# Loading the first batch in order of use, and keeping six partial sums of the first weight open while the values slip in between

## The chip, the cores and the metric

The kernel runs on one core of one Trainium2 chip; the other cores are idle. The metric is the device time of the whole kernel in microseconds (us). The time of one run lies about 1.8 us above the span of the profile, which goes from the first to the last instruction. Time before: 408.8 us, the median of three runs (408.26 to 409.0).

The change touches only the first 45 us.

## The reference, cut to what matters

Linformer attention, then a feed-forward layer with the maximum over three products:

```python
k_proj = einsum('ks,bhsd->bhkd', E, k)        # E, F: 64 x 1024
v_proj = einsum('ks,bhsd->bhkd', F, v)        # q, k, v: 8 x 8 x 1024 x 64
attn   = softmax(q @ k_proj.T / sqrt(64))
x      = (attn @ v_proj), heads side by side  # 8192 x 512
h      = max(x @ w1, x @ w2, x @ w3)          # 512 x 768 each
out    = h @ w_out                            # 768 x 512
```

All inputs and outputs are float32.

## The kernel before

The operands of every matmul are held in bf16; sums and maxima stay in float32. Each load of q, k, v and of the weights changes float32 to bf16 on the way. The Trainium skill ("DMA: Bandwidth & Descriptors", section "SWDGE vs HWDGE vs iDMA") says that a cast during a DMA is to be had from GpSimd only. The kernel keeps to this: all such loads are issued by GpSimd and stand in one queue, q0, with 28.31 MB written. In the trace of the kernel before, the loads of the first batch land in the order in which they are issued (the first at 6.2 us, k of the next batch at 43.4 us). That order is a matter of choice.

The work goes batch by batch (8), each in two chunks of 512 rows. In the first chunk of the first batch TensorE waits for loads; later everything is there in time. w1, w2, w3 are the three weights; each comes in two halves of its rows, that is of the contraction (`ct` 0, 1 and `ct` 2, 3). A column tile `jt` (6 of them) needs 4 matmuls per weight, one for each `ct`. Before, the loads were issued like this (the calls are shortened):

```python
    load_q(LO, first half)      # q, heads 0-3
    load_kv(1, LO)              # k, heads 0-3
    load_kv(2, 0:2); load_kv(2, 2:4)          # v, first two pairs of heads
    make_identity(nc, ident)
    load_w(0, 0)                # first half of w1
    load_q(HI, first half); load_kv(1, HI)    # q and k, heads 4-7
    load_w(1, 0)                # first half of w2
    load_kv(2, V2); load_kv(2, V3)            # v, last two pairs
    load_w(1, 1); load_w(0, 1)  # second halves of w2, of w1
    load_w(2, 0); load_w(2, 1)  # w3
    load_q(ALL, rest)           # q for the second chunk
    # ... w_out, then k of batch 1
```

The first chunk follows that order. TensorE attends to heads 0 to 3 and does `ct` 0 and 1 of w1. It copies these half sums out of PSUM, attends to heads 4 to 7, and does most of w2. Then it returns to w1, and the half sums are added on VectorE, or copied by ScalarE and added by GpSimd:

```python
        for ct in range(2):
            for jt in jts:
                up_mm(h[jt][0], 0, 0, 0, jt, (ct,), last=1)
                if ct == 1:
                    copy("sv"[jt % 2], s1[:, jt], *h[jt])
        then(0)                 # attention of heads 4-7
        # ... w2, ct 0 to 2, into six banks
        for jt in jts:
            t, ns = bank()
            up_mm(t, 0, 0, 0, jt, (2, 3), first=2)
            # ... add to s1; w2, ct 3; maximum
        for jt in jts:
            t, ns = bank()
            up_mm(t, 2, 0, 0, jt, range(NCT))       # w3
            most(hTs[0, 0][:, jt, :], t, ns, s1[:, jt])
            then(5 + jt)        # 5, 6: transposes of the rest of q
```

`idle(n)` issues n warm-up matmuls on zeroes. PSUM is the memory into which TensorE writes its sums; its 8 banks are dealt one at a time (`bank`) or as an aligned pair (`two`). The other names in the code: `q_duo` and `qp` transpose q, `k_pair` and `v_pair` project k and v, `scores` and `exps` are the product of q and k and its exponential, `z` makes the inverse of the softmax sums, `x` multiplies with v and scales. The number in brackets is a pair of heads (for `q_duo` two pairs). `then(key)` does the work that is listed under that key.

The softmax here doesn't subtract the row's maximum and nothing guards it: scores larger than these inputs give would overflow.

## Time and profile before

| | before |
|---|---|
| time, median of 3 runs | 408.8 us |
| span of the profiled run | 407.8 us |
| TensorE busy | 393.8 us (97%) |
| TensorE idle in 0 to 35 us | 6.2 us |
| casting queue | about 206 GB/s written, unbroken from 9 us to beyond 43 us |

Of the page of the kernel before: the span, the busy time of the engines, and the clock that was granted to TensorE in 40 slices, in tenths.

```profile
span 407.8 us, 6116 instructions
...
PE 393.8 (97%) x2452; PEld 180.4 (44%) x2497; DVE 202.3 (50%) x311; ACT 192.9 (47%) x281; POOL 34.9 (9%) x46
...
PEclk9899999999999999999999999999999999999999
```

TensorE (PE) is what is full.

Stretches of 5 us of the kernel before: the stretch, its length, then busy time and number of instructions of PE, weight loads, VectorE, ScalarE, GpSimd, then the granted clock, the DMA share and GB/s written.

```profile
25.00:30.00 5.00, 3.93 (x38) 1.83 (x38) 1.97 (x4) 0.01 (x1) 0.00 (x0) 1.00 1.19 206
30.00:35.00 5.00, 5.00 (x26) 2.13 (x27) 4.10 (x7) 1.77 (x3) 2.97 (x3) 1.00 1.33 204
35.00:40.00 5.00, 4.95 (x54) 2.29 (x54) 5.00 (x9) 1.09 (x2) 2.63 (x3) 1.00 1.24 207
```

From 30 us on TensorE has hardly a gap. So only the time at which it gets there can change.

The timeline of PE of the kernel before (start, duration, line, operation, shapes, count; in brackets the idle time before it and what ended that). L406 projects k, L460 is the up product, L288 projects v, L299 transposes q:

```profile
10.51 0.69 PE L406 MATMUL banks<-efT,k_t 128*64 128x64 bf16 x32 [1.61 <-DMA k_t<-in_k_dram]
...
16.45 2.76 PE L460 MATMUL banks<-xT,w_sb 128*128 128x512 bf16 x11
...
27.46 0.64 PE L288 MATMUL banks<-v_t,efT 128*64 128x128 bf16 x16 [0.80 <-DVE xT L257]
...
29.02 5.92 PE L460 MATMUL banks<-xT,w_sb 128*128 128x512 bf16 x25
34.88 0.64 PE L299 MATMUL banks<-ident,q_t 128*64 128x128 bf16 x16
```

Three things are to be seen. TensorE waits 1.61 us for the first half of k. At 27.46 us it waits 0.80 us for VectorE, because six banks are taken and the remaining pair is still being read. And the first transposes of the rest of q, which stand behind the first column tile of w3, begin when that tile is done, at 34.9 us.

The granted clock comes in stretches of 3.41 us. The two around 12.5 us, of the kernel before (the clock is the column after GpSimd):

```profile
9.08:12.49 3.41, 1.47 (x44) 1.12 (x45) 0.45 (x2) 0.86 (x2) 1.19 (x2) 1.00 1.23 208
12.49:15.91 3.42, 3.33 (x45) 2.02 (x41) 1.03 (x3) 2.59 (x5) 1.67 (x3) 0.50 1.29 201
```

A stretch in which TensorE worked for 1.47 us is followed by one at half clock.

The chain of waits of the same run (start, duration, what):

```profile
18.38 1.89 DVE s L99 x3
20.27 0.39 DVE qT L99
...
20.79 0.23 DVE kpT L99
21.01 0.04 issue
21.05 0.43 PE banks L207 x8
```

Three of the six copies of half sums are done by VectorE, ahead of what the attention of heads 4 to 7 needs from it. In the timeline TensorE waits 0.46 us for VectorE at 21.05 us.

### The profile page before, as it was taken

Reading aid. Unit: us, or ns where it says so; the run is one execution under the profiler, and the core shown is the slowest. Engines: PE = TensorE matmul, PEld = TensorE weight load, DVE = VectorE, ACT = ScalarE, POOL = GpSimd, SP = SyncE. Lnnn points to the kernel's source line nnn. Section 1 sums busy time; section 2 is a strip of 40 time slices with the busy share of each in tenths; the row PEclk is TensorE's granted clock in tenths of the full one; section 3 lists DMA queues with packets and bytes.
Section 4 is the critical chain, followed back from the end, with each engine's and each line's share of the span. In section 5 each row is a group of like instructions: output and inputs, shape, how many; then the busy total and the mean of one; then the engine's idle time right before and its main releaser. Section 6 shows DMA issues by size and latency. Waiting matters only on the chain.

```text
span 407.8 us, 6116 instructions
## 1 busy us (share of the span) xinstructions
PE 393.8 (97%) x2452; PEld 180.4 (44%) x2497; DVE 202.3 (50%) x311; ACT 192.9 (47%) x281; POOL 34.9 (9%) x46
## 2 busy tenths in 40 slices
PE   7879999999999999999999999999999999999995
PEld 2534454344444544444544445444544444444443
DVE  1429665473465527636453565525464363525251
ACT  2432537623764266547445555537535555432322
POOL 7325002002000200200010002000000000000000
PEclk9899999999999999999999999999999999999999
DMA  9999939959926994893799109960520202020202
GB/s 152 206 207 206 220 98 145 251 122 127 244 42 161 191 247 123 121 242 54 182 184 204 52 13 243 203 161 0 123 87 0 104 2 103 2 103 0 104 0 104
DMA packets 58492, 52.30 MB, mean 128 GB/s; under 512 B 25952, under 2 KB 54112, under 8 KB 58464
## 3 DMA queue, kind: packets, MB, share of 16 engines
q0 software_dynamic: 28496, 28.31, 43.8%
q1 hardware_dynamic: 29824, 23.46, 17.9%
q8 instruction: 19, 0.31, 0.3%
q10 hardware_dynamic: 144, 0.13, 0.1%
q14 instruction: 9, 0.07, 0.1%
HBM read 57.15 MB, written 16.78 MB: 181 GB/s over the span
## 4 chain that ended last, share of the span: by engine, by line
PE 91%; DMA 3%; ACT 2%; DVE 2%; issue 1%; POOL 0%; ACTq 0%; DVEq 0%; POOLq 0%
PE banks L460 60%; PE banks L586 19%; PE banks L227 4%; PE banks L288 4%; DMA k_t<-in_k_dram 2%; PE banks L207 2%; PE banks L299 1%; ACT zl L240 1%; DVE xT L257 1%; ACT pT L218 1%; DMA out_dram<-o_sb 0%; DVE s L99 0%; ACT zi L246 0%; DVE m L551 0%; ACT o_sb L99 0%
## 5 line engine op out<-in xcount | busy, mean ns | idle before, releaser
L460 PE MATMUL banks<-xT,w_sb 128*128 128x512 bf16 x1118 | 255.1, 379 | 2.1 <-issue 0.5
L460 PEld LDWEIGHTS <-w_sb 128*128 128x128 bf16 x1152 | 109.4, 98 | 137.0 <-issue 10.7
L551 DVE TENSOR_TENSOR m<-banks,h1s 128x512 f32<-128x512 f32 x90 | 62.0, 689 | 86.1 <-ACT h1s L547 54.7
L547 ACT COPY h1s<-banks 128x512 f32<-128x512 f32 x90 | 52.5, 583 | 92.5 <-PE banks L460 89.2
L586 PE MATMUL banks<-wout_sb,hT 128*128 128x512 bf16 x369 | 84.8, 379 | 0.7 <-DVE hT L470 0.2
L257 DVE TENSOR_TENSOR xT<-banks,zi 128x1024 bf16<-128x1024 f32 (+1 forms) x36 | 39.8, 1106 | 78.4 <-ACT zi L246 53.7
L470 DVE TENSOR_TENSOR hT<-banks,m 128x512 bf16<-128x512 f32 x90 | 62.3, 692 | 10.1 <-PE banks L227 0.5
L99 ACT COPY o_sb<-banks 128x512 f32<-128x512 f32 (+1 forms) x60 | 34.9, 581 | 53.0 <-PE banks L586 53.0
L586 PEld LDWEIGHTS <-hT 128*128 128x128 bf16 x378 | 36.0, 98 | 45.5 <-issue 3.1
L240 ACT ACTIVATE zl<-banks 128x1024 f32<-128x1024 f32 (+1 forms) x36 | 33.5, 931 | 30.8 <-PE banks L227 30.6
L218 ACT ACTIVATE pT<-banks 128x1024 bf16<-128x1024 f32 (+1 forms) x36 | 33.2, 931 | 9.7 <-PE banks L207 9.7
L246 ACT ACTIVATE zi<-zl 128x1024 f32<-128x1024 f32 (+1 forms) x36 | 34.6, 962 | 1.1
L196 POOL DMA_DIRECT2D q_t<-in_q_dram x7 | 6.2, 883 | 194.1 <-DMA qT<-q_p 72.1
L288 PEld LDWEIGHTS <-efT 128*64 128x64 bf16 x288 | 14.5, 116 | 4.5 <-issue 4.1
L227 PE MATMUL banks<-pT,ones 64*64 64x512 bf16 (+1 forms) x144 | 14.0, 379 | 1.5 <-ACT pT L218 0.9
L207 PE MATMUL banks<-qT,kpT 64*64 64x512 bf16 (+1 forms) x144 | 13.1, 360 | 0.9 <-DVE kpT L99 0.5
L227 PE MATMUL banks<-pT,vp 64*64 64x512 bf16 (+1 forms) x144 | 13.4, 359 | 0.4 <-DVE vp L99 0.4
L99 DVE CAST vp<-banks 64x256 bf16<-64x256 f32 (+1 forms) x18 | 7.1, 397 | 10.7 <-PE banks L288 7.1
L288 PE MATMUL banks<-v_t,efT 128*64 128x256 bf16 (+1 forms) x176 | 10.7, 271 | 0.9 <-DVE xT L257 0.8
L227 PEld LDWEIGHTS <-ones 64*64 64x64 bf16 x144 | 4.5, 103 | 15.4 <-issue 15.3
L99 ACT CAST vp<-banks 64x256 bf16<-64x256 f32 x14 | 5.1, 365 | 7.3 <-PE banks L288 7.1
L99 DVE COPY q_p<-q_t 128x1024 bf16<-128x1024 bf16 x24 | 8.5, 419 | 0.0
(47 smaller groups left out, 106.7 us busy)
## 6 DMA issues: line engine op xcount, KB each, us to landing
out_dram<-o_sb SPq DMA_DIRECT2D x30, 512.0 KB, 3.1
k_t<-in_k_dram POOLq DMA_DIRECT2D x7, 1024.0 KB, 14.0
q_t<-in_q_dram POOLq DMA_DIRECT2D x7, 1024.0 KB, 9.6
v_t<-in_v_dram POOLq DMA_DIRECT2D x7, 1024.0 KB, 18.5
w_sb<-in_moe_w_dram POOLq DMA_DIRECT2D x6, 384.0 KB, 14.8
k_t<-in_k_dram POOLq DMA_DIRECT2D x2, 512.0 KB, 11.0
v_t<-in_v_dram POOLq DMA_DIRECT2D x4, 256.0 KB, 11.5
wout_sb<-in_moe_w_out_dram POOLq DMA_DIRECT2D x1, 768.0 KB, 16.3
```

Source lines behind the costliest of these rows:

```text
L99: done = {"v": nc.vector.tensor_copy, "s": nc.scalar.copy, "g": nc.gpsimd.tensor_copy}[eng](out=o, in_=i)
L218: nc.scalar.activation(out=pTs[b, g, lo], in_=t, func=AF.Exp, scale=scale)
L227: nc.tensor.matmul(out=t[hp * HALF:(hp + 1) * HALF, c, 0:nsi * HALF], lhsT=w(rows, hp), rhs=p[rows, hp, :], start=True, stop=True,)
L240: nc.scalar.activation(out=zl, in_=t, func=AF.Ln)
L246: nc.scalar.activation(out=zi, in_=zl, func=AF.Exp, scale=-1.0)
L257: nc.vector.tensor_tensor(out=xTs[b][:, g, lo:lo + nsi, :].rearrange("a (c s) p -> a c (s p)", c=2), in0=t, in1=zi, op=ALU.mult,)
L288: nc.tensor.matmul(out=t[hh * HALF:(hh + 1) * HALF, 0:width], lhsT=efT[:, si, kv - 1, :], rhs=qkv[b][kv][:, heads[hh], si, :], start=(si = ...
L460: nc.tensor.matmul(out=h, lhsT=w_sb[i][:, ct, jt * P:(jt + 1) * P], rhs=xTs[b][:, ct, ch * SPC:(ch + 1) * SPC, :], start=(ct == first), st ...
L470: nc.vector.tensor_tensor(out=o, in0=h, in1=other, op=ALU.max)
L547: nc.scalar.copy(out=h1s, in_=h[0][0])
L551: nc.vector.tensor_tensor(out=m12, in0=h[1][0], in1=h1s, op=ALU.max)
L586: nc.tensor.matmul(out=o_ps, lhsT=hTs[b, ch][:, jt, tt * P:(tt + 1) * P], rhs=wout_sb[:, jt, :], start=(jt == 0), stop=(jt == NJT - 1),)
```

## The change

The intent: let all attention inputs come first, so that the attention of all eight heads is done before the up product starts. Then w1 can run through in one go, with its six banks open over all four `ct`, without copies of half sums, additions or a second visit; the six copies are made of the full sums of w1 at its end instead. The last two pairs of v, and what of the softmax depends on them, slip in between its `ct` steps while the second half of w1 is on its way. The diff, cut to its core:

```diff
     load_q(LO, slice(0, SPC))
     load_kv(1, LO)
+    load_q(HI, slice(0, SPC))
+    load_kv(1, HI)
     load_kv(2, slice(0, 2))
     load_kv(2, slice(2, 4))
 # ... cut
     load_w(0, 0)
-    load_q(HI, slice(0, SPC))
-    load_kv(1, HI)
-    load_w(1, 0)
     load_kv(2, V2)
     load_kv(2, V3)
+    load_w(0, 1)
+    load_w(1, 0)
     load_w(1, 1)
-    load_w(0, 1)
     load_w(2, 0)
+    load_q(ALL, slice(SPC, SI))
     load_w(2, 1)
-    load_q(ALL, slice(SPC, SI))
 # ... cut: k of batch 1 is issued with the rest of its loads, but first
-    for g in range(2):
+    for g in (0, 1):
         exps(0, g, *C0, scores(0, g, *C0))
+    idle(2)
+    z(0)
+    q_duo(1)
+    z(1)
+    idle(2)
+    k_pair(2)
+    k_pair(3)
+    for g in (2, 3):
+        exps(0, g, *C0, scores(0, g, *C0))
     idle(1)
-    z(0)
     v_pair(0)
-    z(1)
-    idle(1)
+    z(2)
     x(0)
     v_pair(1)
+    z(3)
     x(1)
 # ... cut: the old up_first
+        for ct in range(NCT):
             for jt in jts:
-                up_mm(h[jt][0], 1, 0, 0, jt, (ct,))
+                up_mm(h[jt][0], 0, 0, 0, jt, (ct,))
+                if ct == NCT - 1:
+                    copy("sv"[jt % 2], hs[:, jt], *h[jt])
+                if jt == 2 or jt == NJT - 1:
+                    then((0, ct, jt))
+        for i in (1, 2):
+            for jt in jts:
+                t, ns = bank()
+                up_mm(t, i, 0, 0, jt, range(NCT))
+                most(hs[:, jt] if i == 1 else hTs[0, 0][:, jt, :], t, ns, hs[:, jt])
+                then((i, jt))
 # ... cut
-                    1: [lambda: v_pair(2)],
-                    2: [lambda: x(2), lambda: v_pair(3)],
-                    3: [lambda: x(3)],
-                    5: [qp(0, (0, 1), *c1)],
-                    6: [qp(0, (2, 3), *c1)],
+                    (0, 1, 2): [lambda: v_pair(2)],
+                    (0, 1, 5): [lambda: x(2), lambda: v_pair(3)],
+                    (0, 2, 2): [lambda: x(3)],
+                    (2, 0): [qp(0, (0, 1), *c1)],
+                    (2, 1): [qp(0, (2, 3), *c1)],
```

Before, the rest of q came behind all of w3; after, it comes ahead of w3's second half.

More of the change, by code (lines that the diff above doesn't have):

```diff
@@ L169 @@
     load_w(0, 0)
-    load_q(HI, slice(0, SPC))
-    load_kv(1, HI)
-    load_w(1, 0)
     load_kv(2, V2)
     load_kv(2, V3)
+    load_w(0, 1)
+    load_w(1, 0)
     load_w(1, 1)
-    load_w(0, 1)
     load_w(2, 0)
+    load_q(ALL, slice(SPC, SI))
     load_w(2, 1)
-    load_q(ALL, slice(SPC, SI))
     nc.gpsimd.dma_start(out=wout_sb, in_=moe_w_out.rearrange("(jt p) m -> p jt m", p=P))
-    def load_k1():
-        nonlocal k_t1
-        k_t1 = loads.tile([P, H, SI, D], BF16, name="k_t")
-        nc.gpsimd.dma_start(out=k_t1, in_=view(k, 1))
-    k_t1 = None
     def load(b):
         tiles = tuple(
-            loads.tile([P, H, SI, D], BF16, name=nm) if b > 1 or i != 1 else k_t1
-            for i, nm in enumerate(("q_t", "k_t", "v_t"))
+            loads.tile([P, H, SI, D], BF16, name=nm) for nm in ("q_t", "k_t", "v_t")
         )
         qkv[b] = tiles
-        for i in ((0, 2) if b == 1 else (0, 1, 2)):
+        for i in ((1, 0, 2) if b == 1 else (0, 1, 2)):
             dma = nc.gpsimd.dma_start(out=tiles[i], in_=view((q, k, v)[i], b))
@@ L431, with z, x @@
     C0 = (0, SPC)
+    def z(g):
+        invert(0, g, *C0, sums(0, g, *C0))
+    def x(g):
+        scale_x(0, g, *C0, values(0, g, *C0))
     idle(11)
@@ L437 @@
     k_pair(1)
-    for g in range(2):
+    for g in (0, 1):
         exps(0, g, *C0, scores(0, g, *C0))
-    def z(g):
-        invert(0, g, *C0, sums(0, g, *C0))
-    def x(g):
-        scale_x(0, g, *C0, values(0, g, *C0))
+    idle(2)
[7 more added lines that the diff above has]
+        exps(0, g, *C0, scores(0, g, *C0))
     idle(1)
-    z(0)
     v_pair(0)
-    z(1)
-    idle(1)
+    z(2)
     x(0)
     v_pair(1)
+    z(3)
     x(1)
@@ L479, in then @@
                 f()
-        s1 = ffn_sb.tile([P, NJT, CHUNK], FP32, name="s1", bufs=1)
-        s2 = ffn_sb.tile([P, NJT, CHUNK], FP32, name="s2", bufs=1)
+        hs = ffn_sb.tile([P, NJT, CHUNK], FP32, name="hs", bufs=1)
         hTs[0, 0] = ffn_sb.tile([P, NJT, CHUNK], BF16, name="hT")
         jts = range(NJT)
-        def six():
-            return [(t[:, n], ns[n:n + 1]) for t, ns in (two(), two(), two()) for n in (0, 1)]
-        h = six()
-        for ct in range(2):
+        h = [(t[:, n], ns[n:n + 1]) for t, ns in (two(), two(), two()) for n in (0, 1)]
@@ L491, in up_first @@
+        for ct in range(NCT):
             for jt in jts:
-                up_mm(h[jt][0], 0, 0, 0, jt, (ct,), last=1)
-                if ct == 1:
-                    copy("sv"[jt % 2], s1[:, jt], *h[jt])
-        then(0)
-        load_k1()
-        h = six()
-        for ct in range(2):
-            for jt in jts:
-                up_mm(h[jt][0], 1, 0, 0, jt, (ct,))
-            then(1 + ct)
-        for jt in jts:
-            up_mm(h[jt][0], 1, 0, 0, jt, (2,))
-            if jt == 2:
-                then(3)
@@ L506, in up_first @@
-        for jt in jts:
-            t, ns = bank()
-            up_mm(t, 0, 0, 0, jt, (2, 3), first=2)
-            if jt % 2:
-                copy("s", s2[:, jt], t, ns)
-                nc.gpsimd.tensor_tensor(
-                    out=s1[:, jt], in0=s1[:, jt], in1=s2[:, jt], op=ALU.add
-                )
-                added = clock["s"] + 1.3
-            else:
-                nc.vector.tensor_tensor(out=s1[:, jt], in0=t, in1=s1[:, jt], op=ALU.add)
-                added = runs("v", clock["pe"], 0.69, ns)
-            up_mm(h[jt][0], 1, 0, 0, jt, (3,))
-            if jt % 2 == 0:
-                most(s1[:, jt], *h[jt], s1[:, jt], added)
-            elif jt > 2:
-                most(s1[:, jt - 2], *h[jt - 2], s1[:, jt - 2], last)
-            if jt % 2:
-                last = added
@@ L525, in up_first @@
-        most(s1[:, 5], *h[5], s1[:, 5], last)
-        then(4)
-        for jt in jts:
-            t, ns = bank()
-            up_mm(t, 2, 0, 0, jt, range(NCT))
-            most(hTs[0, 0][:, jt, :], t, ns, s1[:, jt])
-            then(5 + jt)
+                up_mm(h[jt][0], 0, 0, 0, jt, (ct,))
[4 more added lines that the diff above has]
+        for i in (1, 2):
+            for jt in jts:
+                t, ns = bank()
+                up_mm(t, i, 0, 0, jt, range(NCT))
+                most(hs[:, jt] if i == 1 else hTs[0, 0][:, jt, :], t, ns, hs[:, jt])
+                then((i, jt))
@@ L673 @@
                 c1 = (SPC, SPC)
-                def attend():
-                    q_duo(1)
-                    k_pair(2)
-                    k_pair(3)
-                    for g in (2, 3):
-                        exps(0, g, *C0, scores(0, g, *C0))
-                    idle(2)
-                    for g in (2, 3):
-                        z(g)
-                up_first({
-                    0: [attend],
-                    1: [lambda: v_pair(2)],
-                    2: [lambda: x(2), lambda: v_pair(3)],
-                    3: [lambda: x(3)],
-                    5: [qp(0, (0, 1), *c1)],
-                    6: [qp(0, (2, 3), *c1)],
-                    7: [sc(0, 0, *c1)],
-                    8: [sc(0, 1, *c1)],
-                    10: [za(0, 0, *c1), sc(0, 2, *c1)],
+                up_first({
+                    (0, 1, 2): [lambda: v_pair(2)],
[3 more added lines that the diff above has]
+                    (2, 1): [qp(0, (2, 3), *c1)],
+                    (2, 2): [sc(0, 0, *c1)],
+                    (2, 3): [sc(0, 1, *c1)],
+                    (2, 5): [za(0, 0, *c1), sc(0, 2, *c1)],
                 })
```

## The prediction

> **What bounds the kernel now.** From about 29 to 402 us TensorE is dense: the page has PE busy 393.8 of 407.8 us, and the table of stretches shows 4.85 to 5.0 us of each 5 us from 30 us to 65 us. Behind the first stage nothing is changed but bank numbers. So only the moment when TensorE can run without gaps can move.
>
> Before that the casting queue binds: the DMA view shows about 206 GB/s (written bytes) unbroken from 9 to beyond 43 us. Landings (issue plus time to landing): q low 6.2, k low 10.5, v0 11.7, v1 13.0, first half of w1 14.9, q high 16.4, k high 19.9, first of w2 21.7, v2 23.1, v3 24.3, second of w2 26.2, second of w1 28.1, w3 30.0 and 31.9, rest of q 34.5, w_out 38.3, next k 43.4. TensorE idles 6.2 us in 0 to 35 us (stretches), 1.6 of it before the first k projection. In the timeline the first column tile of w3 ends at 34.95 us.
>
> **What changes.** No byte and no up matmul goes (72 before and after); warm-up matmuls 21, then 22 (+0.2 us). Removed: three VectorE adds (0.69 us each), three ScalarE copies (0.59) and three GpSimd adds (3.9 in all), off the chain. k, q and v come before the weights: w1's first half moves from 14.9 to about 19 us (2.49 MB instead of 1.70 MB, at 206 GB/s).
>
> **New order, estimated from these durations.** k high lands at 14.3 to 15.3; softmax of groups 2 and 3 (ScalarE 0.6 us a step) ends by about 18; v0, v1 at 16 to 17; w1's first steps start at 19 to 19.5. v2 (20.3), v3 (21.6) and w1's second half (23.5) are slipped in; only one bank pair is left, so v_pair(3) waits 0.8 us for VectorE, as now. w1 ends near 27.3. w2's second half lands at 28.1, so TensorE waits 0.5 us; w2 ends near 32.9. w3's second half, now behind the rest of q, lands where the rest of q does now, 34.5 us: the bytes in front are the same. w3's first tile ends at 34.5 + 2 x 0.216 + 0.05 = 35.0 us, against 34.95. The remaining work is the same.
>
> So the early gain is given back to one weight half: about 0, perhaps 0.3 us from a less loaded VectorE (5.0 of 5.0 us busy in 35 to 40 us now).
>
> **The clock.** The Trainium skill ("TensorE: Matmul & The Clock Gate", Part 1) says activity in a free-running window of about 3.4 us sets full or half clock. The trace agrees: 9.1 to 12.5 us has 1.53 us of PE work, and 12.5 to 15.9 us ran at 0.5. I expect one or two such windows after; 1.6 us of slack before w3's second half absorbs a second.
>
> **Prediction: 408.6 us, 407.3 to 410.3. Faster by over 2%: 0.01; within 2%: 0.98; slower by over 2%: 0.01.**
>
> **What would show it.** First up matmul near 19 us (16.45 now); w1 done near 27; PE waits of 0.5 us at 28 and of 1 to 1.5 us for w_sb ending near 34.5; w3's first tile ending at 34.5 to 35.3; next k at 43.4; PE busy unchanged within 2 us.
>
> **What would make it wrong.** Landings 1 us earlier (they trail the byte count by 1.4 us up to 15 us, 2.4 us later): up to 1 us faster. Two half-clock windows after 19 us, or bank waits in w1: 1 to 2 us slower.

## The result, and the profile after

| | before | after |
|---|---|---|
| time, median (4 runs each, same chip) | 408.53 us (407.98 to 409.0) | 409.19 us (408.23 to 409.37) |
| ratio after to before, 95% interval | | 1.0012 (0.9991 to 1.0033) |
| span of the profiled run | 407.8 us | 407.6 us |
| TensorE busy | 393.8 us | 393.5 us |

A ratio here is the mean time of one kernel's runs over that of the other's in the same rounds, so it isn't quite the ratio of the medians. Executions over 1.5% slower than the fastest of the same kernel are left out of the means. The time is the same within the noise.

Of the page of the kernel after:

```profile
span 407.6 us, 6112 instructions
...
PE 393.5 (97%) x2453; PEld 179.7 (44%) x2498; DVE 201.6 (49%) x308; ACT 191.1 (47%) x278; POOL 31.1 (8%) x43
...
PEclk9999999999999999999999999999999999999999
```

The clock reads 9 in every slice although one stretch was at half clock, as is shown below: it lies across two slices and takes less than a tenth from each. VectorE, ScalarE and GpSimd each lost a little work (0.7, 1.8 and 3.8 us): the additions and what feeds them. In the chain of the kernel before, there is nothing but TensorE from 30 to 41 us, and there these were done, so they were off the way. TensorE has the same work. Stretches of 5 us of the kernel after, columns as before:

```profile
25.00:30.00 5.00, 4.73 (x30) 2.02 (x26) 3.32 (x6) 1.56 (x3) 0.00 (x0) 1.00 1.31 203
30.00:35.00 5.00, 5.00 (x37) 2.34 (x35) 4.04 (x7) 0.00 (x0) 0.00 (x0) 1.00 1.22 207
35.00:40.00 5.00, 4.84 (x44) 2.14 (x42) 3.53 (x6) 1.19 (x2) 1.75 (x2) 1.00 1.25 210
```

The timeline of PE of the kernel after (L398 projects k, L461 is the up product, L280 projects v, L291 transposes q):

```profile
9.04 0.70 PE L398 MATMUL banks<-efT,k_t 128*64 128x64 bf16 x32
...
16.64 0.64 PE L280 MATMUL banks<-v_t,efT 128*64 128x128 bf16 x16 [0.81 <-DMA v_t<-in_v_dram]
...
18.39 0.50 PE L461 MATMUL banks<-xT,w_sb 128*128 128x512 bf16 x1 [0.43 <-DMA w_sb<-in_moe_w_dram]
19.11 3.09 PE L461 MATMUL banks<-xT,w_sb 128*128 128x512 bf16 x7 [0.22 <-ACT zi L238]
...
24.54 0.64 PE L280 MATMUL banks<-v_t,efT 128*64 128x128 bf16 x16 [0.80 <-DVE xT L249]
...
26.32 8.21 PE L461 MATMUL banks<-xT,w_sb 128*128 128x512 bf16 x36 [0.16 <-issue]
34.46 0.64 PE L291 MATMUL banks<-ident,q_t 128*64 128x128 bf16 x16
```

The first up matmul comes 1.94 us later than before (18.39 against 16.45 us), and the transposes behind the first tile of w3 come 0.42 us earlier (34.46 against 34.88 us). From there on the two traces run in parallel: the first matmul of the down product stands at 41.67 us before and at 41.26 us after, one of the last batch at 400.4 and 400.0 us, and wherever a matmul of one trace was matched with its like in the other (some 1900 of them) the difference was 0.40 or 0.41 us. So on TensorE nothing behind the first chunk gives or takes any time. The spans differ by 0.25 us only, because what follows the last matmul took 4.18 us after and 4.03 us before.

But two things don't fit. The profiled pair says that after is 0.2 us faster in span, while the timed runs have it 0.7 us slower in the median. And the wait that I had predicted, 1 to 1.5 us for w3's second half, isn't there: this half landed at 32.98 us, and TensorE asked for it at 33.94 us. Something else had held TensorE back. Two adjoining stretches of the kernel after show what:

```profile
15.13:18.54 3.41, 1.80 (x33) 1.03 (x30) 1.80 (x4) 2.12 (x4) 0.90 (x1) 1.00 1.20 204
18.54:21.96 3.42, 3.20 (x8) 1.06 (x7) 0.17 (x1) 0.34 (x1) 2.00 (x3) 0.50 1.18 210
```

The half clock, which before fell on the attention of the first heads, now fell on the first steps of w1: they came every 0.43 us in place of 0.216 us.

### The profile page after: what moved, and what is told of

Same layout as the page of the kernel before. It is cut to its first block, busy times and chain, and to the rows that moved or that the text cites. A ratio compares the mean times of both kernels' runs of the same rounds, so it can differ in the third digit from the quotient of the medians.

```text
span 407.6 us, 6112 instructions
## 1 busy us (share of the span) xinstructions
PE 393.5 (97%) x2453; PEld 179.7 (44%) x2498; DVE 201.6 (49%) x308; ACT 191.1 (47%) x278; POOL 31.1 (8%) x43
## 4 chain that ended last, share of the span: by engine, by line
PE 90%; DMA 3%; ACT 2%; DVE 1%; POOL 1%; issue 1%; DVEq 0%; ACTq 0%; POOLq 0%
PE banks L461 61%; PE banks L553 19%; PE banks L219 4%; PE banks L280 4%; DMA w_sb<-in_moe_w_dram 3%; PE banks L199 2%; PE banks L291 1%; DVE xT L249 1%; DMA out_dram<-o_sb 0%; ACT zi L238 0%; ACT zl L232 0%; POOL k_t L143 0%; ACT pT L210 0%; POOL q_t L148 0%; POOL v_t L143 0%
## 5 line engine op out<-in xcount | busy, mean ns | idle before, releaser
L461 PE MATMUL banks<-xT,w_sb 128*128 128x512 bf16 x1118 | 256.2, 381 | 2.8 <-issue 0.6
L461 PEld LDWEIGHTS <-w_sb 128*128 128x128 bf16 x1152 | 109.7, 98 | 138.6 <-issue 12.4
L280 PEld LDWEIGHTS <-efT 128*64 128x64 bf16 x288 | 13.8, 110 | 5.5 <-issue 5.2
L99 DVE CAST vp<-banks 64x256 bf16<-64x256 f32 (+1 forms) x18 | 7.1, 397 | 10.5 <-PE banks L280 5.6
L280 PE MATMUL banks<-v_t,efT 128*64 128x256 bf16 (+1 forms) x176 | 9.9, 254 | 1.9 <-DMA v_t<-in_v_dram 0.8
```

The source lines that it names most:

```text
L99: done = {"v": nc.vector.tensor_copy, "s": nc.scalar.copy, "g": nc.gpsimd.tensor_copy}[eng](out=o, in_=i)
L280: nc.tensor.matmul(out=t[hh * HALF:(hh + 1) * HALF, 0:width], lhsT=efT[:, si, kv - 1, :], rhs=qkv[b][kv][:, heads[hh], si, :], start=(si = ...
L461: nc.tensor.matmul(out=h, lhsT=w_sb[i][:, ct, jt * P:(jt + 1) * P], rhs=xTs[b][:, ct, ch * SPC:(ch + 1) * SPC, :], start=(ct == first), st ...
```

## The experiments

Two theories. **W** (the prediction): what TensorE waits for is w3's second half, because the rest of q was put ahead of it. **F**: the chain through the first weight is what counts, that is its late first half, the half clock and the single free pair of banks; w3's second half has slack. All runs gave correct results. They were made in four groups. The runs of a group shared a chip and the runs of before: both kernels once more and w3 later and earlier; each part alone, the late load with warm-up matmuls, and the first timing of a version meant to gain; the kernel after with warm-up matmuls and that version with and without them; the kernel before with more of them. Times are compared inside a group.

### Both kernels once more

No edit. What was expected of the kernel before:

> The kernel before, unchanged, to see what belongs to the kernel and what to the run. If the late landing of the first k half (10.5 us, against 9.0 us in the kernel after) comes from the order of the loads, it lands at 10.2 to 10.8 us again and the half-clock stretch lies at 12.5 to 15.9 us; if it is chance of the run, the landing moves towards 9.0 us. Time 407.9 to 409.1 us; first column tile of w3 done within 0.5 us of 34.95 us.

and of the kernel after:

> The kernel after, unchanged. Theory W (my prediction: the second half of w3 is what TensorE waits for): in some runs a PE wait for w_sb ends near 33 to 34.5 us. Theory F (the chain through the first weight is what counts: late first half of w1, a half-clock stretch over its first steps, the one bank pair): no such wait, PE gapless from 27 us on, w3's first tile done at about 34.5 us. Time 408.2 to 409.4 us.

Measured: before 408.75 us (407.93 to 409.9), after 409.22 us (408.84 to 409.42); the shared median of before was 408.92 us. In the new profile of before k landed at 10.5 us again and the half clock lay at 12.6 to 16.0 us again. In the new profile of after k landed at 10.8 us, not at 9.0 us: the landing is chance of the run, not a matter of the order (with the old order it came at 9.5 us in a later run). There was no half clock except in the last microsecond of the run. And there the predicted wait stands, in the timeline of PE of this second run of the kernel after:

```profile
19.22 2.12 PE L461 MATMUL banks<-xT,w_sb 128*128 128x512 bf16 x9 [0.19 <-DMA w_sb<-in_moe_w_dram]
...
25.25 8.00 PE L461 MATMUL banks<-xT,w_sb 128*128 128x512 bf16 x35
33.87 0.60 PE L461 MATMUL banks<-xT,w_sb 128*128 128x512 bf16 x2 [0.62 <-DMA w_sb<-in_moe_w_dram]
```

and in the chain of waits of the same run (start, duration, what):

```profile
19.46 14.36 DMA w_sb<-in_moe_w_dram
33.82 0.05 issue
33.87 0.60 PE banks L461 x2
```

The load was issued at 19.46 us and landed at 33.82 us, and TensorE went on 0.05 us later. So the two runs of one kernel have two different limits. In one the clock was halved and TensorE came to the third step of w3's first tile at 33.94 us by itself. In the other the clock was full, TensorE came 0.62 us too early, and the load let it go at 33.87 us. Both theories are right, each in one run, and both give the same time to within 0.1 us.

### w3's second half later, and earlier

Later: w_out goes ahead of it.

```diff
     load_w(2, 0)
     load_q(ALL, slice(SPC, SI))
-    load_w(2, 1)
     nc.gpsimd.dma_start(out=wout_sb, ...)
+    load_w(2, 1)
```

> The kernel after with w_out ahead of w3's second half, so that this half lands near 36.8 us instead of 33.0 us. Both theories expect a PE wait that ends there and a later end. Theory W (no slack now): the whole 3.8 us arrives, about 412.6 us. Theory F (third step of w3's first tile began 0.95 us after the landing): 2.8 to 3.0 us arrive, about 411.7 us, and the later matmuls are all shifted by one constant.

Measured: 414.78 us (414.37 to 415.69), ratio to before 1.0143. The wait is where both theories want it. In the timeline of PE of this kernel:

```profile
37.23 1.03 PE L461 MATMUL banks<-xT,w_sb 128*128 128x512 bf16 x2 [4.45 <-DMA w_sb<-in_moe_w_dram]
```

The landing at 37.18 us is 3.36 us later than in the second run of after, but the first down matmul is 5.47 us later (46.67 against 41.20 us). Both expectations were too small. The stretches of this kernel say where to look:

```profile
31.65:35.06 3.41, 1.14 (x6) 0.29 (x3) 1.33 (x2) 0.00 (x0) 0.00 (x0) 1.00 1.22 209
35.06:38.47 3.41, 1.24 (x8) 0.41 (x10) 0.17 (x1) 0.00 (x0) 0.00 (x0) 0.50 1.22 207
38.47:41.88 3.41, 3.41 (x36) 1.80 (x32) 1.91 (x3) 0.00 (x0) 0.00 (x0) 0.50 0.90 149
```

The long wait brought two stretches at half clock, the second of them over work that was full. To test this, the same kernel with warm-up matmuls in the wait:

```diff
+                    (1, 5): [lambda: idle(18)],
                     (2, 0): [qp(0, (0, 1), *c1)],
```

> The late load of w3's second half again, with 18 warm-up matmuls (3.9 us) in the 4.45 us in which TensorE waited. The late load gave 5.5 us where 3.3 us of landing were to be expected. If the other 2.1 us were the two half-clock stretches behind the wait (35.1 to 41.9 us), no half clock is granted here and the time is 411.9 to 412.6 us, first down matmul near 44.5 us instead of 46.7 us. If they came from the loads of the next batch behind, it stays at 414.3 us or more.

Measured: 412.66 us (412.54 to 413.22), just above the expected range; the ratio to before is 1.0108, where the late load without warm-up matmuls had 1.0143 in its group; first down matmul at 44.58 us, as expected. Of this kernel, the two stretches again:

```profile
35.06:38.47 3.41, 2.83 (x26) 1.27 (x26) 0.59 (x1) 0.00 (x0) 0.00 (x0) 1.00 1.23 208
38.47:41.88 3.41, 3.36 (x31) 1.40 (x30) 2.68 (x5) 0.60 (x1) 1.63 (x2) 1.00 0.86 145
```

With the clock full the late landing costs 44.58 - 41.20 = 3.38 us, which is what the landing moved (37.20 - 33.82 = 3.38 us). The other 46.67 - 44.58 = 2.09 us were the half clock. So a wait of 4.45 us costs more than 4.45 us of standing still.

Earlier: w3 in one piece, the rest of q behind it.

```diff
     load_w(2, 0)
-    load_q(ALL, slice(SPC, SI))
     load_w(2, 1)
+    load_q(ALL, slice(SPC, SI))
```

> The kernel after with w3's second half ahead of the rest of q: the half lands near 30.4 us, the rest of q near 33.0 us. Theory W: 0.7 to 1.5 us faster, about 407.7 us. Theory F: no change, within 0.3 us, because PE reaches w3 only at 33.5 us and the transposes of q only at 34.5 us.

Measured: 408.28 us (408.07 to 408.74), where the kernel after in the same rounds had 409.22 us; profiled span 406.6 against 407.6 us. So W is right here: the gain over after is 0.9 us. Against before it is the same within the noise (ratio 0.9982, 0.9945 to 1.0019). Only one short wait was left near w3, now for q. In the timeline of PE of this kernel:

```profile
24.84 8.43 PE L461 MATMUL banks<-xT,w_sb 128*128 128x512 bf16 x37
33.45 0.64 PE L291 MATMUL banks<-ident,q_t 128*64 128x128 bf16 x16 [0.18 <-DMA q_t<-in_q_dram]
```

This also shows the size of the swap. In both orders the last load that the first tiles wait for stands behind the same bytes. From its landing to the first down matmul it is 40.25 - 33.40 = 6.85 us here, when that load is q, and 41.20 - 33.82 = 7.38 us in the second run of after, when it is w3's half. The two matmuls of w3's first tile that must still follow, 2 x 0.216 us, make most of the 0.53 us. The rest of the 0.95 us between these two profiles is that the last load landed earlier, at 33.40 against 33.82 us, behind the same bytes. With landings that scatter this much, 0.5 us is what the swap is shown to be worth, and how much of the 0.9 us in the times is chance of four runs each was not separated.

### Each part of the change alone

The order of TensorE of after with the load order of before:

> One part alone: the TensorE order of after with the load order of before. Theory F and W agree that the second half of k (19.6 to 19.9 us) now stands in front of the values and of the first weight, so the first up matmul comes at about 22 to 23 us, w1's second half lands at 28 us, w1 ends near 30.9 us and w3 is reached near 36 us: 2 to 3.5 us slower than after, about 411.5 us. If the rearranged order alone were worth something, it would be no slower than 409.5 us.

and the order of TensorE of before with the load order of after:

> The other part alone: the TensorE order of before with the load order of after. First up matmul at 18 to 19 us, then the second weight's first half (24.7 to 25.5 us) is asked for before w1's second half, so PE waits 1 to 3 us for w_sb near 24.7 us: 1.5 to 3 us slower than before, about 411 us. If the load order alone were worth something, it would be below 408.5 us.

Measured, against a median of 408.3 us of before: 412.84 us (411.74 to 415.58; ratio 1.0119) and 413.25 us (411.75 to 414.35; ratio 1.0116). Each part alone costs 1.2%, more than I expected (about 411.5 and 411 us); only both together cost nothing that the times can tell. The reasons differ in detail from what I expected. In the timeline of PE of the first one:

```profile
15.87 1.06 PE L291 MATMUL banks<-ident,q_t 128*64 128x128 bf16 x16 [3.69 <-DMA q_t<-in_q_dram]
...
24.43 0.61 PE L461 MATMUL banks<-xT,w_sb 128*128 128x512 bf16 x1
```

and of the second one (L288 projects v, L460 is the up product):

```profile
15.44 1.06 PE L288 MATMUL banks<-v_t,efT 128*64 128x128 bf16 x16 [3.04 <-DMA v_t<-in_v_dram]
...
27.49 1.47 PE L460 MATMUL banks<-xT,w_sb 128*128 128x512 bf16 x6
```

In the second the wait isn't for w2 near 24.7 us, as I had written, but for v at 15.4 us, because the load order now has q and k of heads 4 to 7 ahead of v. In both the wait was long enough to bring a run of half clock behind it, 13.65 us from 14.7 us on in the first and 10.24 us from 12.7 us on in the second. How much of the 1.2% is waiting and how much is clock was not separated.

### The clock, in both kernels

The kernel after, with four more warm-up matmuls in its waits:

```diff
     x(0)
+    idle(2)
     v_pair(1)
     z(3)
     x(1)
+    idle(2)
```

> The kernel after with the same four warm-up matmuls. If a half-clock stretch is hidden here behind the landing of w3's second half, no run has a clock below 0.998 but the spans stay at 407.1 to 407.6 us as in its runs at full clock (time 408.8 to 409.4 us), and the profile shows a PE wait for w_sb that ends just after w3's second half lands. If the half clock was what held the kernel after back, it gains 1 us and more (below 408.3 us).

Measured: 409.31 us (408.8 to 409.43), against a median of 408.45 us of before in the same rounds; ratio 1.0019 (1.0005 to 1.0034). All six runs had a mean clock of 0.998 and above and spans of 407.0 to 407.6 us. In the timeline of PE of this kernel (L463 is the up product):

```profile
33.99 0.60 PE L463 MATMUL banks<-xT,w_sb 128*128 128x512 bf16 x2 [0.41 <-DMA w_sb<-in_moe_w_dram]
```

w3's half landed at 33.94 us. So with the clock full the kernel after isn't faster: what the clock gives, the load takes back.

The kernel before, with six more warm-up matmuls ahead of its wait for k:

```diff
     q_duo(0)
-    idle(6)
+    idle(12)
```

> The kernel before with six more warm-up matmuls (1.3 us) in the 1.6 us in which TensorE waits for the first k half, so that the stretch up to 12.5 us, where both profiles of before had only 1.47 us of PE work, has about 2.6 us. If that stretch set the half clock from 12.5 to 15.9 us, no half clock is granted there; the two value projections take 0.64 us instead of 1.06 us and the kernel reaches w3's first tile up to 1 us earlier, where the rest of q (34.3 to 34.5 us) stops it: spans 406.2 to 407.2 us in all runs, none of 407.7 us and more, median 0 to 0.8 us below before. If the added matmuls only take time, nothing changes or it gets slower by up to 0.3 us.

One number in it is wrong: it was the first profile of before that had 1.47 us in the stretch ahead of the half clock; the second had 1.87 us.

Measured: 408.48 us (408.3 to 409.32), against 408.26 us of before in the same rounds; ratio 1.0 (0.9981 to 1.0019). In the time nothing came of it, and one of its six spans, 407.6 us at a clock of 1.0, lies above the expected range. Ten of the eleven runs of before in these rounds had a clock of 0.998 and above anyhow, so there was little half clock to be saved. But the profile is of use: it shows the kernel before at full clock. Its timeline of PE (L460 is the up product, L299 transposes q):

```profile
15.03 2.76 PE L460 MATMUL banks<-xT,w_sb 128*128 128x512 bf16 x12
...
27.71 5.92 PE L460 MATMUL banks<-xT,w_sb 128*128 128x512 bf16 x25
33.56 0.64 PE L299 MATMUL banks<-ident,q_t 128*64 128x128 bf16 x16
```

The span is 406.8 us, 1.0 us less than in the first profile of before, and w3's first tile is done just when the rest of q has landed (33.48 us). The first down matmul comes at 40.36 us, 6.88 us behind that landing, the same distance as in the run with w3 first. In these rounds the eleven spans of before have a median of 406.5 us. The first profile of before, with 407.8 us, was one of its slower runs, and that is why the two profiles had the wrong sign.

### A version meant to gain

w3 ahead of the rest of q, v_pair(2) and x(2) three matmuls earlier so that the pair of banks is free in time, and the transposes one tile later:

```diff
-                    (0, 1, 2): [lambda: v_pair(2)],
-                    (0, 1, 5): [lambda: x(2), lambda: v_pair(3)],
+                    (0, 0, 5): [lambda: v_pair(2)],
+                    (0, 1, 2): [lambda: x(2)],
+                    (0, 1, 5): [lambda: v_pair(3)],
                     (0, 2, 2): [lambda: x(3)],
-                    (2, 0): [qp(0, (0, 1), *c1)],
-                    (2, 1): [qp(0, (2, 3), *c1)],
-                    (2, 2): [sc(0, 0, *c1)],
-                    (2, 3): [sc(0, 1, *c1)],
+                    (2, 1): [qp(0, (0, 1), *c1)],
+                    (2, 2): [qp(0, (2, 3), *c1)],
+                    (2, 3): [sc(0, 0, *c1)],
+                    (2, 4): [sc(0, 1, *c1)],
```

> w3's second half ahead of the rest of q, v_pair(2) and x(2) each three matmuls earlier, so that v_pair(3) doesn't wait 0.8 us for the bank pair, and the transposes of the rest of q one tile later. The next limits are landings: w1's second half at 23.3 us and the second half of the second weight at 27.0 us, worked out from the run with w3 first: third step of w1 at 23.35 us instead of 23.85 us, w3 reached 0.4 us earlier than there. Theory of close limits: 0.3 to 0.5 us faster than that run (span about 406.2 us at full clock, 407.8 us in the time), 1.0 to 1.4 us faster than after. If the bank wait alone had counted: 0.8 us faster than that run.

Measured: 408.54 us (407.12 to 409.54), ratio to before 0.9999 (0.9981 to 1.0017): no gain over before in this job. The profiled run was better than expected: span 405.3 us, first down matmul at 39.09 us. But the six runs fell into two groups. Three with a mean clock of 0.998 to 1.0 had spans of 405.3, 405.5 and 406.4 us; three with 0.996 had 407.2, 407.4 and 407.8 us. One half-clock stretch is 3.41 x 0.5 of 407 us, 0.4% of the mean clock, so these three probably had one. No trace of them was kept, so this is inferred. It would mean that without slack at w3 the half clock shows at once: the means of the groups are 405.7 and 407.5 us. So it was tried with the four warm-up matmuls, beside an unchanged control:

> The version with w3 first and the two slips, with two warm-up matmuls in each of the two waits ahead of the first weight (after x(0) and after x(1)). In its last timing three of six runs had a mean clock of 0.996 and spans of 407.2 to 407.8 us, the other three 405.3 to 406.4 us. If those three paid for a half-clock stretch over the first weight's steps, which this kernel has no slack to hide, here no run has a clock below 0.998 and the spans are 405.3 to 406.4 us: time 407.0 to 408.0 us, 0.2 to 0.4% below before. If the added matmuls only add work, it is 0.4 to 0.9 us slower than the kernel without them.

> The version with w3 first and the two slips, unchanged, as the control on the same chip. Runs at a clock of 0.998 and above: spans of 405.3 to 406.4 us; runs at 0.996: 407.2 to 407.8 us; the share of the two is chance, so the median lies anywhere from 407.2 to 409.2 us.

Measured, beside a median of 408.45 us of before: with the warm-up matmuls 407.82 us (407.06 to 408.05), ratio 0.9983 (0.9968 to 0.9997); the control 407.68 us (407.21 to 408.03), ratio 0.9982 (0.9968 to 0.9996). All twelve runs had a clock of 0.998 and above. So the gain over before is about 0.17% in this job, clear of the noise in both; in the job before there was none. Whether the warm-up matmuls prevent the bad group isn't shown: the control had none either. What is shown is that they cost nothing that these rounds can tell. In the timeline of PE of the version with them there is no wait in w3 (L463 is the up product):

```profile
23.62 9.42 PE L463 MATMUL banks<-xT,w_sb 128*128 128x512 bf16 x41
...
33.54 1.04 PE L463 MATMUL banks<-xT,w_sb 128*128 128x512 bf16 x4
```

## Why the prediction was right

The predicted time was 408.6 us (407.3 to 410.3), within 2%; measured were 409.19 us and, in later rounds, 409.22 us. Point by point:

- **Only the first chunk counts.** Right: the shift of 0.40 us between the two profiles stays constant on TensorE to the last batch.
- **The removed copies and additions were off the chain.** Right: VectorE, ScalarE and GpSimd lost 0.7 to 3.8 us of work, and the time didn't follow. What I overlooked is that the copies of half sums, which are moved and not removed, did stand in the chain of before (1.89 us on VectorE, at 18.4 us); to take them off it may be a part of the early gain, which wasn't tested.
- **The early gain is given back to w3's second half, behind the rest of q.** Shown, but not by the profile that came with the result. There a half-clock stretch hid it, with 0.96 us of slack at the half's landing. At full clock the wait is there (0.62 and 0.41 us, ending at 33.87 and 33.99 us), and to put w3 ahead of q gave 0.9 us in the times, of which 0.5 us is accounted for. I had said 1 to 1.5 us, ending near 34.5 us: both terms were too large, since that load landed at 33.0 to 33.9 us.
- **TensorE waits 0.5 us at 28 us for w2's second half.** Wrong: it landed at 26.6 and 27.4 us, and no wait is listed. The landings were taken from the first profile of before, as if they were fixed. k came at 10.5 us there, and at 8.9 to 10.8 us over ten profiles with its place in the order of after. But a late k alone doesn't explain it: in the second run of after k came later than in before, at 10.8 us, and w2's second half still came 0.7 us ahead of the forecast. From k's landing to that landing it took 17.6 us in the first run of after and 16.6 us in the second.
- **A second half-clock stretch is absorbed by slack.** Right in effect, and I had the place wrong: the profiled run had one stretch, at 18.5 to 22.0 us, over w1.
- **About 0 in sum, perhaps 0.3 us gained from a less loaded VectorE.** VectorE gave nothing: from the first transposes of the rest of q to the first down matmul it is 6.79 us before and 6.80 us after, though VectorE was busy for 5.00 of the 5 us before and 3.53 after. The sum was right in size, and probably not in sign; that it came out so close is in part luck. With four more warm-up matmuls after is 0.19% slower than before, with an interval clear of 1. The error lies in what it was compared with: I took 34.95 us from a profile of before that had a half clock in it. At full clock before gets there at 33.6 us. The landing of w3's half, forecast for 34.5 us, came 0.6 to 1.5 us early as well, and in the difference the two errors nearly cancel. What is left is that the work behind w3's half is about 0.5 us longer than that behind the rest of q; two matmuls are 0.43 us of it.

What stays open: why k's landing scatters by nearly 2 us from run to run and the loads behind it by about 1 us more, and what sets the phase of the clock's stretches, which differed in every profile.

## What to carry to other kernels

When a stage is fed by one queue, ask which load stands last behind the same bytes and how much work must follow it; putting the load with the least work behind it last was worth more here (0.5 us in the traces) than all the removed work. Two limits that lie within a microsecond take turns from run to run, so one profile shows one of them: profile the same kernel twice, and look at the granted clock first. A wait of TensorE costs its length and, if it empties a stretch of the clock, the work of the next stretches at half speed on top (2.09 us behind the wait of 4.45 us here); warm-up matmuls in the wait cost nothing measurable here.

## What the Trainium skill lacked or had wrong

- "TensorE: Matmul & The Clock Gate", Part 1, says that the clock falls to half after an idle window of about 3.4 us. In the first 42 us of the profiles here it fell six times, each time after a stretch of 3.41 us that held 0.77 to 1.87 us of PE work; in the first profile of before (1.47 us) no gap of PE was over 1.61 us. Stretches with 2.1 us and more kept it full. Two right at the start of a kernel, with 1.72 and 1.95 us, kept it too, so the bound isn't sharp.
- The same part says that one busy window brings the full clock back. After a half-clock stretch with 3.20 us of PE work (the kernel after) or 3.33 us (before) it did. In the run with the old load order a stretch with 3.28 us at half clock was followed by one more at half clock. Busy time as the profile has it doesn't decide it alone.
- "DMA: Bandwidth & Descriptors" has no figure for the scatter of a landing from run to run. The second load in the queue, under one load order, landed at 8.9 to 10.8 us over ten profiles, and w3's second half, in the three profiles of after and its warm form, at 32.98, 33.82 and 33.94 us.
